# The first weight block of a gated mix of a long convolution and a bilinear unit, brought in as two transfers instead of one

## The chip, the cores and the metric

The kernel runs on one core of a Trainium2 chip. The metric is the device time of one execution in microseconds (us); lower is better. The kernel before was run three times: median 587.12 us, from 586.51 to 587.54.

The core has TensorE (PE, matrix products, with the weight loads shown apart as PEld), VectorE (DVE), ScalarE (ACT), GpSimd (POOL) and SyncE (SP, which mostly issues transfers). Transfers issued by SP, ACT and POOL run on 16 shared DMA engines.

## The reference

For 2048 tokens of 512 channels the reference mixes two branches with a gate per token:

```python
x = A_u
g = _sigmoid((x * gate_w).sum(-1, keepdims=True))
a = _A_ref(x, ...)      # long convolution: y = irfft(rfft(u) * rfft(K)) + u * D_skip
b = _B_ref(x, B_w_gate, B_w_up, B_w_down)
...
g = jnp.einsum("bsd,df->bsf", x, w_gate)
u = jnp.einsum("bsd,df->bsf", x, w_up)
h = g * u
return jnp.einsum("bsf,fd->bsd", h, w_down)
...
return g * a + (1 - g) * b
```

Branch a is a convolution over the whole sequence, with a filter K computed from state-space parameters. Branch b is a bilinear gated unit with 1792 hidden channels. The change concerns the start of branch b.

## The kernel before

**Precision by three products.** TensorE works in a rounded 32-bit format. Each operand is therefore split into a high part (a cast by ACT) and a low part (operand minus high part, by DVE), and each product is three matmuls: high by high, high by low, low by high. `THREE` (line 578) gives their order; for the very first block it is reversed (line 584), so that high by high comes first, then high weights by low tokens (`whi`, `xs`), then low weights by high tokens (`wlo`, `xs`).

**Tiling of branch b.** The 512 channels are four pieces of 128 (`KT` = 4, index `kt`), the 1792 hidden channels are 14 blocks of 128 (index `f`, in four groups), the tokens are four chunks of 512. For a block and a chunk, `hidden` (line 596) forms the gate product in the bank `pg` and the up product in the bank `pu`, each over four values of `kt`. ACT copies `pg` out, DVE multiplies it with `pu` into `h`, ACT and DVE split `h` into `hh` and `hl`, and `down` multiplies these with the down weights into `y`. Transforms for branch a (banks `k`) are fitted between these matmuls, and DVE and ACT compute the tables of the filter meanwhile.

**The start.** `first_loads` (line 492) issues the first transfers. For each `kt` it loads a token tile of 128 channels by 512 tokens (256 KB, into the tile `y`, on SP's queue) and the 128 gate columns and 128 up columns of block 0 that belong to this `kt` (128 KB together, into the tile `ev`, as one transfer). For `kt` = 0 this weight transfer is issued from ACT's queue (line 504), for the others from SP's. Next come the weights of blocks 1 and 2. TensorE meanwhile runs matmuls on zeros (line 514).

`tokens` (line 560) and `first_split` (line 538) turn these into operands. For each `kt`, ACT casts the token tile (512 columns) and then the gate and up weights together (256 columns), and DVE makes the two low parts in the same way. In block 0 the products run by `kt`, gate and up in turn (line 605): `pg` for `kt` = 0 is the first real product of the kernel. `product` (line 580) names the parts of the weight tiles on which it depends, `("k", kt)` for block 0.

**What sets the order.** Nothing is issued as it is written down. Each call of `add` (line 229) makes a task with an engine, an assumed duration in us, the tiles read and written, a rank, an earliest time `after` and, for transfers, a size in KB. `Work.run` (line 301) is a list scheduler: again and again it takes the task that can start first by its own reckoning (ties by rank, then by the order of the calls), and writes the instructions down in that order. Each engine then executes in exactly this order (`InOrder`, line 116) and waits where data are late. For transfers the reckoning uses one shared bus of 0.33 KB per ns, 0.9 us before a transfer begins and 1.0 us until it has landed (lines 214 to 217). A transfer that is issued holds one of a limited number of completion counters; one that finds none free waits on its queue.

Of the kernel before, what the change touches and what calls it, by code (L numbers as in the profile page):

```python
# [10 lines left out]
F32 = mybir.dt.float32  # L11
# [3 lines left out]
ALU = mybir.AluOpType  # L15
# [3 lines left out]
P = 128  # L19
# [150 lines left out]
class Bus:  # L170
# [18 lines left out]
    def add(self, task, at, us):  # L189
        at = max(at, self.now)  # L190
        self.serve(self.queues, self.now, at)
        self.now = at
        self.queues[task.engine == "pool"].append([task, us])
        return self.serve([[[*x] for x in q] for q in self.queues], at, 1e9)
# [170 lines left out]
def gated_mix_kernel(  # L365
# [16 lines left out]
    pe, dve, act, sp, pool_q = (InOrder(tc, e) for e in (nc.tensor, nc.vector, nc.scalar, nc.sync, nc.gpsimd))  # L382
# [3 lines left out]
    add = work.add  # L386
# [18 lines left out]
    def new(pool, tag, shape, dtype=F32, bufs=1, loose=False):  # L405
        return work.tile(pools[pool], tag, shape, dtype, bufs, loose)

    def bank():
        return new("ps_k", "k", [P, D], bufs=4, loose=True)
# [38 lines left out]
    raws = {}  # L448
# [32 lines left out]
    def load_two(key, tile_of, src, one=True):  # L481

        t = tile_of([P, 2, D])
        for k in range(2):
            raws[key(k)] = (t, k)
        if one:
            add("sp", 0.42, lambda: sp.dma_start(t.t, src), w=[t], dma=512, rank=-1)
        return t

    ws, wd, xs = {}, {}, {}  # L490

    def first_loads():
        in_y = lambda shape: new("mid", "y", shape, bufs=2)
        in_ev = lambda shape: new("mid", "ev", shape, bufs=2)
        in_in = lambda shape: new("mid", "in", shape, bufs=2)
        xsrc = lambda kt: xT[P * kt : P * kt + P, :D]
        w0 = raws["w0"] = in_ev([P, 2, D])
        xt = [load_two(lambda k, n=n: ("x", 0, 0, 2 * n + k), in_y, None, False) for n in range(2)]
        wsrc = wts[0][:, : 2 * D].rearrange("p (k d) -> p k d", k=2)
        for kt in range(KT):  # L500

            t, k, ks = xt[kt // 2], kt % 2, slice(P * kt, P * kt + P)
            add("sp", 0.42, lambda t=t, k=k, kt=kt: sp.dma_start(t.t[:, k], xsrc(kt)), w=[(t, k)], dma=256, rank=-1)
            e, q = ("sp", sp) if kt else ("act", act)
            add(e, 0.42, lambda q=q, ks=ks: q.dma_start(w0.t[:, :, ks], wsrc[:, :, ks]), w=[(w0, ("k", kt))], dma=128, rank=-1)
        for f in (1, 2):
            load_two(lambda k, f=f: ("w", f, k), in_ev if f == 1 else in_in, wts[f][:, : 2 * D].rearrange("p (k d) -> p k d", k=2))


        zero = new("glu", "acc", [P, D], bufs=3)  # L510
        scratch = bank()
        add("dve", 0.2, lambda: dve.memset(zero.t, 0.0), w=[zero], rank=-1)

        def warm():
            for _ in range(2):
                pe.matmul(scratch.t, zero.t[:, :P], zero.t, start=True, stop=True)

        add("pe", 3.4, warm, r=[zero], w=[scratch], rank=-1)

    def weights(fs):  # L520
        for f in fs:
            ws[f] = [new("glu", n, [P, 2 * D], F32R, SLOTS) for n in ("whi", "wlo")]
            if f == 0:
                for kt in range(KT):
                    first_split(kt)
                    if kt + 1 < KT:
                        tokens(0, 0, kt + 1)
                continue
            for c in range(2):
                load(("w", f, c), wts[f][:, c * D : (c + 1) * D])  # L530
                if f in GROUPS[0]:
                    split(*ws[f], c, ("w", f, c))
                else:
                    high(ws[f][0], c, ("w", f, c))
            if f not in GROUPS[0]:
                rest(*ws[f], wts[f][:, : 2 * D], 2)

    def first_split(kt):

        hi, lo, t, k = *ws[0], raws["w0"], ("k", kt)  # L540
        cut = lambda x: x.rearrange("p (c d) -> p c d", c=2)[:, :, P * kt : P * kt + P]
        src = lambda: t.t[:, :, P * kt : P * kt + P]
        add("act", 0.38, lambda: act.copy(cut(hi.t), src()), r=[(t, k)], w=[(hi, k)], rank=0)
        add(
            "dve", 0.42,
            lambda: dve.tensor_tensor(out=cut(lo.t), in0=src(), in1=cut(hi.t).bitcast(F32), op=ALU.subtract),
            r=[(t, k), (hi, k)], w=[(lo, k)], rank=0,
        )

    def down_weights(fs):  # L550
        for f in fs:
# [27 lines left out]

    def product(pg, which, w, x, kt, after, first):  # L580
        base = which * D + kt * P
        part = ("k", kt) if first else which

        three = THREE[::-1] if first else THREE

        def fn():
            for n, (a, b) in enumerate(three):
                pe.matmul(
                    pg.t, w[a].t[:, base : base + P], x.t[:, b], start=kt == 0 and n == 0, stop=kt == KT - 1 and n == 2
                )  # L590

        add("pe", 0.681, fn, r=[(w[0], part), (w[1], part), x], w=[pg], rank=2, after=after)
# [3 lines left out]
    def hidden(f):  # L596

        pg = [new("ps_g", n, [P, D]) for n in ("pg", "pu")]
        x = dict(xs)
        after = T_STEP * len(steps) - 5.0  # L600
        steps.append(f)
        pairs = [(which, kt) for which in range(2) for kt in range(KT)]
        if f == 0:

            pairs.sort(key=lambda p: p[1])
        for which, kt in pairs:
            product(pg[which], which, ws[f], x[kt], kt, after, not steps[1:] and f == 0)
        h = new("glu", "h", [P, D])
        hh, hl = (new("glu", n, [P, D], F32R, SLOTS) for n in ("hh", "hl"))
        add("act", 0.59, lambda: act.copy(h.t, pg[0].t), r=[pg[0]], w=[h], rank=0)  # L610
        add(
            "dve", 0.69, lambda: dve.tensor_tensor(out=h.t, in0=pg[1].t, in1=h.t, op=ALU.mult),
            r=[pg[1], h], w=[h], rank=0,
        )
        add("act", 0.62, lambda: act.copy(hh.t, h.t), r=[h], w=[hh], rank=0)
        add(
            "dve", 0.69,
            lambda: dve.tensor_tensor(out=hl.t, in0=h.t, in1=hh.t.bitcast(F32), op=ALU.subtract),
            r=[h, hh], w=[hl], rank=0,
        )  # L620
        return hh, hl
# [391 lines left out]
    def x_table(b):  # L1013

        x, ri, (su, di) = xtab[b], ris[b], sus[b]
        ps = new("tab", "ps", [P, TB, 4])
        lead = [(x, ("l", k)) for k in range(3)]
        tt(0.26, lambda: ps.t, lambda: x.t[:, 0, :, 0:4], lambda: x.t[:, 1, :, 0:4], ALU.add, lead, [ps])
        outer(
            x, lambda: x.t[:, :, :, 0:4], lambda: ps.t, lambda: ri.t[:, :, :, W_M],  # L1020
            lambda: su.t[:, :, W_M], lambda: di.t[:, :, 4:11], [*lead, ps, ri, su, di],
        )
        return x
# [384 lines left out]


    first_loads()  # L1410
    prologue()
    for t in range(NR // 4):
# [7 lines left out]
    x = x_table(0)  # L1420
    for b in range(NB):
# [5 lines left out]
        if b + 1 < NB:  # L1427
            direct_powers(b + 1)
            leads(b + 1)
            x = x_table(b + 1)  # L1430
# [59 lines left out]
```

## Time and profile before

| | |
|---|---|
| median of the runs | 587.12 us |
| lowest, highest of three | 586.51, 587.54 us |
| the profiled execution, its own time | 588.43 us |
| span of the profiled execution | 586.6 us |
| TensorE busy | 576.4 us (98%) |
| VectorE busy | 511.3 us (87%) |
| ScalarE busy | 399.0 us (68%) |
| GpSimd busy | 113.4 us (19%) |
| moved by DMA | 136.28 MB, mean 232 GB/s |

The profile is of one execution. Its span runs from the first to the last instruction that the profiler recorded; the device time is a little longer. The chain of waits is followed back from the last instruction, at each step to what released it. In the timeline, each row gives start, duration, engine, line, operation, output and inputs, and in brackets how long the engine sat idle before and what ended that. Nearly all instructions are recorded at line 124, the helper that issues them, so they are told apart by their tiles: `xs` are token operands (high and low part in one tile), `whi` and `wlo` the high and low weights, `ev` the raw weights of the first blocks, `y` at the start the raw token tiles (later it is also the name of other buffers, among them the results of `down`).

### The profile page before, as it was taken

What the parts mean: (1) busy time and instruction counts of PE and PEld (TensorE: products, weight loads), DVE (VectorE), ACT (ScalarE), POOL (GpSimd) and SP (SyncE); (2) the same over time, 40 slices, a digit from 0 to 9 for tenths busy, and PEclk for the clock granted to TensorE, in tenths of its full rate; (3) what the DMA queues carried; (4) which work ended last, traced back from release to release, by engine and by line L of the source; (5) the groups of instructions that cost most, each with busy time, mean ns of one, the idle gap of its engine ahead of it and who ended that gap; (6) DMA issues with size and microseconds to landing.
All of it is one profiled execution on the core that took longest, in us unless ns stands there. A gap on an engine that the chain in (4) does not pass through costs nothing.

```text
span 586.6 us, 14827 instructions
## 1 busy us (share of the span) xinstructions
PE 576.4 (98%) x5996; PEld 433.9 (74%) x5996; DVE 511.3 (87%) x812; ACT 399.0 (68%) x891; POOL 113.4 (19%) x159
## 2 busy tenths in 40 slices
PE   8999999999989999999999999999999999999997
PEld 5777777877876777887777778777878787677775
DVE  6998999999999999999799999995999982367664
ACT  5468888898578589876968764899696523443351
POOL 0002222311102231310412200421321104011011
PEclk9999999999999999999999999999999999999999
DMA  8999969997647698998697859899958349899976
GB/s 276 383 369 357 374 241 319 289 257 212 125 154 181 194 272 205 228 245 297 135 257 249 183 180 304 158 187 276 221 136 212 65 143 230 290 270 253 283 159 125
DMA packets 71687, 136.28 MB, mean 232 GB/s; under 512 B 6852, under 2 KB 35780, under 8 KB 69188
## 3 DMA queue, kind: packets, MB, share of 16 engines
q1 hardware_dynamic: 47668, 87.10, 43.0%
q0 software_dynamic: 23392, 47.98, 39.5%
q8 instruction: 47, 0.77, 0.6%
q10 hardware_dynamic: 560, 0.26, 0.2%
q14 instruction: 20, 0.16, 0.1%
HBM read 80.27 MB, written 55.05 MB: 231 GB/s over the span
## 4 chain that ended last, share of the span: by engine, by line
PE 83%; DVE 6%; ACT 4%; DMA 4%; issue 1%; SPq 0%; DVEq 0%; ACTq 0%
PE pg L124 23%; PE pu L124 23%; PE y L124 22%; PE k L124 16%; DVE v L124 1%; DMA pb<-par_d 1%; DMA xs_d<-xs 1%; DVE x L124 1%; DMA y<-in_xT 1%; DMA xs<-xs_d 1%; ACT acc L124 1%; DVE t L124 1%; ACT ev L124 1%; ACT xs L124 1%; ACT e L124 1%
## 5 line engine op out<-in xcount | busy, mean ns | idle before, releaser
L124 PE MATMUL pg<-xs,whi 128*128 128x512 f32 x448 | 138.9, 391 | 1.0 <-DVE xs L124 0.6
L124 PE MATMUL pu<-xs,whi 128*128 128x512 f32 x448 | 138.3, 390 | 0.0
L124 PEld LDWEIGHTS pg<-xs,whi 128*128 128x128 f32 x448 | 84.2, 188 | 20.2 <-ACT whi L124 2.0
L124 PEld LDWEIGHTS pu<-xs,whi 128*128 128x128 f32 x448 | 84.2, 188 | 16.9
L124 PE MATMUL y<-dhi,hl 128*128 128x512 f32 x224 | 90.3, 403 | 2.9 <-DVE hl L124 2.4
L124 PE MATMUL pu<-xs,wlo 128*128 128x512 f32 x224 | 90.1, 402 | 0.0
L124 PE MATMUL pg<-xs,wlo 128*128 128x512 f32 x224 | 89.4, 399 | 0.4 <-ACT h L124 0.4
L124 PE MATMUL y<-dlo,hh 128*128 128x512 f32 x224 | 87.5, 391 | 0.0
L124 PE MATMUL y<-dhi,hh 128*128 128x512 f32 x224 | 87.3, 390 | 0.0
L124 POOL DMA_DIRECT2D out<-acc x44 | 40.2, 968 | 180.4 <-ACT acc L124 173.0
L124 ACT COPY ev<-k 128x512 f32<-128x512 f32 x112 | 58.8, 596 | 14.5 <-PE k L124 14.4
L124 ACT CAST hh<-h 128x512 fp32r<-128x512 f32 x56 | 34.6, 618 | 45.7 <-DVE h L124 45.5
L124 PEld LDWEIGHTS y<-dhi,hl 128*128 128x128 f32 x224 | 42.0, 187 | 24.4 <-issue 8.1
L124 DVE TENSOR_TENSOR h<-pu,h 128x512 f32<-128x512 f32 x56 | 38.5, 688 | 23.6 <-PE pu L124 23.0
L124 PEld LDWEIGHTS pu<-xs,wlo 128*128 128x128 f32 x224 | 42.0, 187 | 20.0 <-issue 10.7
L124 ACT ACTIVATE acc<-y,ngate 128x512 f32<-128x512 f32 x62 | 41.7, 685 | 21.9 <-PE y L124 18.9
L124 PEld LDWEIGHTS pg<-xs,wlo 128*128 128x128 f32 x224 | 42.1, 188 | 18.4 <-issue 6.9
L124 ACT COPY h<-pg 128x512 f32<-128x512 f32 x56 | 32.9, 587 | 28.3 <-PE pg L124 22.0
L124 PEld LDWEIGHTS y<-dhi,hh 128*128 128x128 f32 x224 | 42.1, 188 | 9.1
L124 PEld LDWEIGHTS y<-dlo,hh 128*128 128x128 f32 x224 | 42.1, 188 | 8.2 <-DVE dlo L124 0.3
L124 DVE TENSOR_TENSOR hl<-h,hh 128x512 fp32r<-128x512 f32 x56 | 38.4, 686 | 3.0 <-ACT hh L124 2.7
L124 PEld LDWEIGHTS k<-v,x 128*32 128x32 f32 x2048 | 30.6, 109 | 6.4 <-issue 4.7
(130 smaller groups left out, 965.4 us busy)
## 6 DMA issues: line engine op xcount, KB each, us to landing
xs<-xs_d SPq DMA_DIRECT2D x36, 512.0 KB, 5.8
out<-acc POOLq DMA_DIRECT2D x44, 256.0 KB, 5.9
raw<-in_wts SPq DMA_DIRECT2D x33, 256.0 KB, 5.6
xs_d<-xs SPq DMA_DIRECT2D x16, 512.0 KB, 6.6
su_d<-ev POOLq DMA_DIRECT2D x32, 256.0 KB, 6.3
y_d<-ts SPq DMA_DIRECT2D x28, 256.0 KB, 4.9
in<-su_d POOLq DMA_DIRECT2D x12, 512.0 KB, 5.9
sk_d<-ev SPq DMA_DIRECT2D x6, 1024.0 KB, 5.4
```

Of the source, the lines that this page charges most:

```text
L124: got = getattr(self.engine, name)(*args, **kw)
```

## The change

For `kt` = 0 the transfer of 128 KB from ACT's queue is replaced by two of 64 KB. The gate columns are issued first, from ACT's queue; the token tile follows from SP's queue; the up columns come behind it, from SP's queue too. The values of `after` (0.0, 0.1, 0.2) fix this order for the planner. Each of the two halves has its own cast on ACT (128 columns, assumed 0.27 us) and its own low part on DVE (128 columns, assumed 0.29 us), and the products of `kt` = 0 depend on their own half only. For `kt` = 1 to 3 everything is as before.

```diff
         for kt in range(KT):
...
-            add("sp", 0.42, lambda t=t, k=k, kt=kt: sp.dma_start(t.t[:, k], xsrc(kt)), w=[(t, k)], dma=256, rank=-1)
-            e, q = ("sp", sp) if kt else ("act", act)
-            add(e, 0.42, lambda q=q, ks=ks: q.dma_start(w0.t[:, :, ks], wsrc[:, :, ks]), w=[(w0, ("k", kt))], dma=128, rank=-1)
+            x_in = lambda t=t, k=k, kt=kt: sp.dma_start(t.t[:, k], xsrc(kt))
+            if kt == 0:
+                for c in range(2):
+                    e, q = ("sp", sp) if c else ("act", act)
+                    add(
+                        e, 0.42, lambda q=q, c=c, ks=ks: q.dma_start(w0.t[:, c, ks], wsrc[:, c, ks]),
+                        w=[(w0, ("k", kt, c))], dma=64, rank=-1, after=0.2 * c,
+                    )
+                    if c == 0:
+                        add("sp", 0.42, x_in, w=[(t, k)], dma=256, rank=-1, after=0.1)
+                continue
+            add("sp", 0.42, x_in, w=[(t, k)], dma=256, rank=-1)
+            add("sp", 0.42, lambda ks=ks: sp.dma_start(w0.t[:, :, ks], wsrc[:, :, ks]), w=[(w0, ("k", kt))], dma=128, rank=-1)
...
-        hi, lo, t, k = *ws[0], raws["w0"], ("k", kt)
-        cut = lambda x: x.rearrange("p (c d) -> p c d", c=2)[:, :, P * kt : P * kt + P]
-        src = lambda: t.t[:, :, P * kt : P * kt + P]
-        add("act", 0.38, lambda: act.copy(cut(hi.t), src()), r=[(t, k)], w=[(hi, k)], rank=0)
...
+        hi, lo, t = *ws[0], raws["w0"]
+        for c in [slice(0, 2)] if kt else [slice(0, 1), slice(1, 2)]:
+            k = ("k", kt) if kt else ("k", kt, c.start)
+            cut = lambda x, c=c: x.rearrange("p (c d) -> p c d", c=2)[:, c, P * kt : P * kt + P]
+            src = lambda c=c: t.t[:, c, P * kt : P * kt + P]
+            add("act", 0.38 if kt else 0.27, lambda cut=cut, src=src: act.copy(cut(hi.t), src()), r=[(t, k)], w=[(hi, k)], rank=0)
+            add(
+                "dve", 0.42 if kt else 0.29,
+                lambda cut=cut, src=src: dve.tensor_tensor(
+                    out=cut(lo.t), in0=src(), in1=cut(hi.t).bitcast(F32), op=ALU.subtract
+                ),
+                r=[(t, k), (hi, k)], w=[(lo, k)], rank=0,
+            )
...
-        part = ("k", kt) if first else which
+        part = which if not first else ("k", kt) if kt else ("k", kt, which)
```

More of the change, by code (lines that the diff above doesn't have):

```diff
@@ L538, in first_split @@
     def first_split(kt):
-        hi, lo, t, k = *ws[0], raws["w0"], ("k", kt)
-        cut = lambda x: x.rearrange("p (c d) -> p c d", c=2)[:, :, P * kt : P * kt + P]
-        src = lambda: t.t[:, :, P * kt : P * kt + P]
-        add("act", 0.38, lambda: act.copy(cut(hi.t), src()), r=[(t, k)], w=[(hi, k)], rank=0)
[L544 to L548, printed above, removed]
+        hi, lo, t = *ws[0], raws["w0"]
[11 more added lines that the diff above has]
+            )
     def down_weights(fs):
```

## The prediction

> **What bounds the kernel now.** I read the page first, for the engine that fills the span and for the share of the chain that ended last.
>
> ```profile
> span 586.6 us, 14827 instructions
> ...
> PE 576.4 (98%) x5996; PEld 433.9 (74%) x5996; DVE 511.3 (87%) x812; ACT 399.0 (68%) x891; POOL 113.4 (19%) x159
> ...
> PE 83%; DVE 6%; ACT 4%; DMA 4%; issue 1%; SPq 0%; DVEq 0%; ACTq 0%
> ```
>
> TensorE is busy for 98% of the span and carries 83% of the chain. A change at the very start can therefore pay only by letting the dense part of TensorE's work begin earlier, and only if no later wait eats the lead. So I went to the chain in order of time, over the first 70 us, to see what the dense part hangs on.
>
> ```profile
> 0.74 3.95 DMA y<-in_xT
> ...
> 5.69 1.45 PE pg L124 x3
> 7.14 0.69 PE pu L124 x3
> ```
>
> The chain begins with the first token tile (`y<-in_xT`), which lands 3.95 us after its issue, and reaches the first three matmuls at 5.69. These take 1.45 us, the next three 0.69: there are 0.76 us of slack in the first triple, and the first block's gate and up weights are what the change touches. The timeline of the first microseconds shows the instructions (start, duration, engine, operation, and in brackets the idle time before).
>
> ```profile
> 0.74 0.47 ACTq L124 DMA_DIRECT2D ev<-in_wts  x1
> ...
> 0.74 0.86 SPq L124 DMA_DIRECT2D y<-in_xT  x2
> ...
> 1.66 0.43 SPq L124 DMA_DIRECT2D ev<-in_wts  x1
> ...
> 2.12 0.47 SPq L124 DMA_DIRECT2D y<-in_xT  x1
> ...
> 2.63 0.43 SPq L124 DMA_DIRECT2D ev<-in_wts  x1
> ...
> 3.11 0.47 SPq L124 DMA_DIRECT2D y<-in_xT  x1
> ...
> 4.71 0.62 ACT L124 CAST xs<-y 128x512 fp32r<-128x512 f32 x1 [1.68 <-DMA y<-in_xT]
> 5.08 0.89 SPq L124 DMA_DIRECT2D ev<-in_wts  x2
> 5.24 0.40 ACT L124 CAST whi<-ev 128x256 fp32r<-128x256 f32 x1
> 5.36 0.69 DVE L124 TENSOR_TENSOR xs<-y,xs 128x512 fp32r<-128x512 f32 x1 [3.80 <-ACT xs L124]
> ...
> 5.81 0.62 ACT L124 CAST xs<-y 128x512 fp32r<-128x512 f32 x1 [0.17 <-DMA y<-in_xT]
> 5.97 0.42 DVE L124 TENSOR_TENSOR wlo<-ev,whi 128x256 fp32r<-128x256 f32 x1
> ...
> 6.46 0.69 DVE L124 TENSOR_TENSOR xs<-y,xs 128x512 fp32r<-128x512 f32 x1
> ```
>
> ACT casts the token tile (4.71 to 5.33), then gate and up weights together (5.24 to 5.64), and TensorE starts at 5.69. DVE makes the tokens' low part (5.36 to 6.05) and then the weights' low part (5.97 to 6.39). Because each product runs high by high, high weights by low tokens, low weights by high tokens, the second matmul needs the tokens' low part. The timeline of TensorE in narrow windows gives the single instructions.
>
> ```profile
> 5.69 0.80 PE L124 MATMUL pg<-xs,whi 128*128 128x512 f32 x1 [0.45 <-ACT whi L124]
> 6.11 0.29 PEld L124 LDWEIGHTS pg<-xs,whi 128*128 128x128 f32 x1
> 6.28 0.62 PE L124 MATMUL pg<-xs,whi 128*128 128x512 f32 x1
> 6.44 0.28 PEld L124 LDWEIGHTS pg<-xs,wlo 128*128 128x128 f32 x1
> 6.71 0.43 PE L124 MATMUL pg<-xs,wlo 128*128 128x512 f32 x1
> 6.98 0.40 PE L124 MATMUL pu<-xs,whi 128*128 128x512 f32 x1
> ```
>
> The second weight load starts at 6.11, 0.06 after the tokens' low part is finished (6.05); the third at 6.44, 0.05 after the weights' low part (6.39). The matmuls start at 6.28, 6.71 and 6.98: spaced 0.43, then 0.27 us.
>
> **The change, part by part.** *First matmul.* It needs the gate's high part and the tokens' high part, and no longer the up half. The sizes of one cast on ACT are 0.62 for 512 columns and 0.40 for 256, so an estimate for 128 is 0.40 - 0.11 = 0.29; on DVE, 0.69 and 0.42 give 0.42 - 0.135, again 0.29. If the gate's cast is out of the way when the token tile lands, TensorE starts 0.04 after 5.33, at 5.37: 0.32 earlier.
>
> *Second matmul.* Its weight load still waits for 6.05, hence 6.11, and the start is still 6.28. The 0.32 us are thus gained in front of a wait that the change does not touch: worth 0. *Third matmul.* Its low part is now ready early, but the matmul follows the second by 0.43, and its weight load at 6.44 lay before 6.71 already: worth 0, unless the array takes its faster pace sooner. If the spacings 0.43 and 0.27 both became the 0.23 of the three-matmul step (0.69 / 3), that would be 0.20 + 0.04 = 0.24 us. Bounds 0 to -0.24; I take 0, since the row at 6.11 does not move.
>
> [...]
>
> *ACT's order.* The order is fixed by the planner. By its constants (0.33 KB per ns, 0.9 to start, 1.0 to land) the gate half is planned to land ahead of the token tile, so its cast is put in front of the token cast. Whether that is free depends on when the gate half really lands. The transfers of the two queues in the first 3.5 and the first 4.25 us, and landing times counted from the issue:
>
> ```profile
> q1 hardware_dynamic: 134, 0.26, 38.1%
> q10 hardware_dynamic: 117, 0.06, 6.6%
> ...
> q1 hardware_dynamic: 210, 0.39, 41.3%
> q10 hardware_dynamic: 265, 0.12, 10.7%
> ...
> ev<-in_wts ACTq DMA_DIRECT2D x1, 128.0 KB, 4.3
> ```
>
> q10 is ACT's queue, q1 SP's. By 3.5 us SP's queue had moved about the first token tile (0.26 MB) and ACT's 117 packets, 0.06 MB: the size of the new gate half. So the gate half would finish with the token tile, not well ahead of it. If it lands 0.29 before 4.69 its cast is free; if together, it puts off the token cast by 0.29 less the 0.09 by which ACT's instructions overlap (4.71 + 0.62 against 5.24), 0.20; at the latest it lands where the whole 128 KB did, 0.74 + 4.3 = 5.04, and the delay is 0.35 + 0.20 = 0.55. All of this passes through the tokens' low part to the second matmul. I take +0.1, between "just ahead" and "together".
>
> *The up half, and the second cast and low part.* The extra cast costs 2 x 0.29 - 0.40 = 0.18 on ACT, and 0.16 on DVE. ACT's part falls before 4.71 (idle 1.68) and between 5.24 and 5.81 (idle 0.17); DVE's first part in its 3.80 of idle time, its second ends 0.13 earlier than the present 6.39, before 6.46. Nothing waits longer: 0. If the cover were gone, it would be 0.18.
>
> *The issue moved onto SP.* One more issue of 0.43 goes between the first token tile and the second, so that every later transfer on SP is issued later. Byte for byte the queues carry the same, and the second token tile still follows the same 384 KB. There is one hard wait, though: after the issue at 3.11 SP pauses until 5.08.
>
> ```profile
> SPq L124 <- DMA ev<-in_wts: 1.9, 2, 1.5
> ...
> DMA to landing us min/median/max: 3.4/4.5/4.8
> ```
>
> The longest of these waits, 1.5, is this pause, and it ends 0.04 after the first weights land (5.04). Six transfers on SP and two on ACT had been issued: the ninth waits for the first. With the extra transfer the ninth is no longer the fourth weights but the fourth token tile. Its issue moves from 3.11 to about 4.7 (the first landing). What that costs is not in the trace; the weights' landing times bound it: 4.7 + 3.4 = 8.1, or 4.7 + 4.8 = 9.5.
>
> ```profile
> 8.14 0.62 ACT L124 CAST xs<-y 128x512 fp32r<-128x512 f32 x1 [0.17 <-DMA y<-in_xT]
> ...
> 9.53 0.42 DVE L124 TENSOR_TENSOR wlo<-ev,whi 128x256 fp32r<-128x256 f32 x1
> ...
> 10.62 0.19 PEld L124 LDWEIGHTS pg<-xs,wlo 128*128 128x128 f32 x1
> ```
>
> Today that tile's cast starts at 8.14; the last product that hangs on it is ready at 9.95 and needed at 10.62. So 0.67 us of lateness is covered; 1.4 late would cost 0.7. Bounds 0 to +0.7. The fourth weights were issued at 5.08, with the same queue ahead, and met the shortest landing at the earliest; I take 0.
>
> [...]
>
> *The order behind it.* The planner decides every later step by comparing start times; some change by a few hundredths to 0.4 us, so neighbours can change places far behind the start. The places where TensorE stood idle show what that can be worth.
>
> ```profile
> 26.86 0.73 PE L124 MATMUL pg<-xs,whi 128*128 128x512 f32 x2 [0.57 <-DVE xs L124]
> ...
> 142.35 0.50 PE L124 MATMUL y<-dhi,hl 128*128 128x512 f32 x1 [0.74 <-DVE hl L124]
> ...
> 173.91 0.50 PE L124 MATMUL y<-dhi,hl 128*128 128x512 f32 x1 [1.63 <-DVE hl L124]
> ...
> 20.00:142.00 122.00, 120.21 (x842) 89.94 (x840) 118.45 (x201) 101.09 (x228) 25.31 (x41) 1.00 0.92 305
> ```
>
> From 20 to 142 us TensorE is busy for 120.21 of 122 and DVE (third figure) for 118.45. A lead of tenths can vanish in any of these three waits, and the largest, 1.63, is the size of what one changed place can open or close. Bounds -1.63 to +1.63; I take 0, having no row for either sign.
>
> *Sum:* 0 + 0 + 0.1 + 0 + 0 + 0 = +0.1 us. The profiled execution took 588.43 (span 586.6 and 1.83 around it), 1.31 above the median of the runs, 587.12. So 588.5 profiled, and a median of 587.2.
>
> **The rivals.** *A, the early start is kept:* the gate half lands early, and the whole 0.32 stays, because the second matmul is not held by the tokens' low part. For it: the second matmul also comes one 0.43 step after the first's streaming began. Against it: the row at 6.11. Time 587.12 - 0.32 = 586.8. *B, the start gets worse:* the gate half lands last (+0.55), or the fourth token tile comes late (+0.7); one of the two, 587.7 to 587.8. For it: the packet counts, and the pause on SP. Against it: the 0.67 of cover. *C, faster:* the new order closes the wait at 173.91. For it: it is a wait for one DVE step, which the order places. Time 587.2 - 1.63 = 585.6. *D, slower:* the new order opens another such wait. The place is a low part of the hidden values (`hl`) behind another DVE step, while DVE is full and TensorE has nothing else in its fixed order; it decides as soon as that step is later than the last matmul ahead of it, as at 142.35 and 173.91. Price up to 1.63: 588.8. Against C and D: a change of a few tenths may leave the order nearly as it was.
>
> **How the numbers follow.** The forecast gets 0.43, A 0.12, B 0.12, C 0.15, D 0.18; D gets a little more than C since two such waits have arisen where DVE is full. About 0.2%, 1.17 us, is what a measurement of this kernel can tell from no change. The forecast, A and B lie within it: same 0.67, faster 0.15, slower 0.18. The range goes from C's 585.6 to D's 588.8, which takes in the bounds of the start; of C and D the outer part, some 0.2, lies outside.
>
> **What would show it right or wrong.** Right: the first matmul near 5.4 to 5.6 while the second stays at 6.2 to 6.5; two casts and two low parts of 0.29 for the first weights; SP's pause in front of the fourth token tile instead of the fourth weights; the first block's last matmul within 0.3 of where it was. Wrong: a second matmul before 6.1 (A); a weight load at 10.6 or later that waits (B); a TensorE wait for `hl` that is gone (C) or new (D) by over 1 us.

## The result, and the profile after

The changed kernel took 591.07 us (median of 7 runs, 589.85 to 595.52) against 587.54 us for the kernel before in the same comparison (7 runs, 586.51 to 590.66): ratio 1.0056, 95% interval 1.003 to 1.0083. By the ratio it is slower by about 3.3 us, by the medians by 3.5: outside the range on record, and well beyond 0.2%.

The page of the changed kernel, in the lines that answer to those of before:

```profile
span 590.7 us, 14832 instructions
...
PE 576.9 (98%) x5996; PEld 435.1 (74%) x5996; DVE 512.1 (87%) x813; ACT 400.1 (68%) x892; POOL 113.6 (19%) x159
...
PE 80%; DVE 9%; ACT 5%; DMA 3%; issue 1%; SPq 0%; DVEq 0%; ACTq 0%
...
L124 PE MATMUL pg<-xs,wlo 128*128 128x512 f32 x224 | 90.5, 404 | 4.5 <-ACT h L124 4.5
```

TensorE is busy for 576.9 us, 0.5 more than before; the span is 4.1 longer. So TensorE mostly waits longer, and the last row says for what: 4.5 us in front of `pg` products, for `h`, ACT's copy that empties the bank `pg`. In the page of before the same row was:

```profile
L124 PE MATMUL pg<-xs,wlo 128*128 128x512 f32 x224 | 89.4, 399 | 0.4 <-ACT h L124 0.4
```

The timeline of the first microseconds shows the first of these waits grow:

```profile
0.74 0.86 SPq L124 DMA_DIRECT2D y<-in_xT  x2
...
1.66 0.90 SPq L124 DMA_DIRECT2D ev<-in_wts  x2
...
4.51 0.33 SPq L124 DMA_DIRECT2D y<-in_xT  x1
4.52 0.30 ACT L124 CAST whi<-ev 128x128 fp32r<-128x128 f32 x1 [1.56 <-DMA ev<-in_wts]
...
5.16 0.62 ACT L124 CAST xs<-y 128x512 fp32r<-128x512 f32 x1 [0.34 <-DMA y<-in_xT]
...
5.83 0.50 PE L124 MATMUL pg<-xs,whi 128*128 128x512 f32 x1 [0.62 <-ACT xs L124]
5.88 0.61 ACT L124 CAST xs<-y 128x512 fp32r<-128x512 f32 x1
...
6.55 0.50 PE L124 MATMUL pg<-xs,whi 128*128 128x512 f32 x1 [0.23 <-DVE xs L124]
...
9.22 0.62 ACT L124 CAST xs<-y 128x512 fp32r<-128x512 f32 x1 [1.59 <-DMA y<-in_xT]
...
12.03 1.14 ACT L124 CAST whi<-ev 128x512 fp32r<-128x512 f32 x2 [1.78 <-DMA ev<-in_wts]
...
13.30 1.14 ACT L124 CAST whi<-in 128x512 fp32r<-128x512 f32 x2
14.35 0.58 ACT L124 COPY h<-pg 128x512 f32<-128x512 f32 x1
...
14.97 0.54 PE L124 MATMUL pg<-xs,wlo 128*128 128x512 f32 x1 [2.83 <-ACT h L124]
```

Four things are to be seen. First, SP issues **two token tiles** before the up part. The first cast of tokens starts at 5.16 instead of 4.71, the second at 5.88 without any wait: the second tile was there already. The description of the change ahead of the prediction says that `after` fixes the order gate, token tile, up part. That is wrong. The second token tile has no earliest time, so the scheduler takes it at 0.0, ahead of the first with its 0.1. Second, the fourth token tile is the ninth transfer, issued at 4.51, and its cast starts at 9.22 (8.14 before). Third, block 1's weights (`ev`, 512 columns) are cast from 12.03 and block 2's (`in`) from 13.30. Fourth, ACT copies `pg` only behind block 2's casts, at 14.35, and TensorE stands for 2.83 us. Before, the same three steps were:

```profile
9.80 1.14 ACT L124 CAST whi<-ev 128x512 fp32r<-128x512 f32 x2 [0.74 <-DMA ev<-in_wts]
11.27 0.59 ACT L124 COPY h<-pg 128x512 f32<-128x512 f32 x1 [0.33 <-PE pg L124]
11.75 1.14 ACT L124 CAST whi<-in 128x512 fp32r<-128x512 f32 x2
```

The copy stood ahead of block 2's casts. In the scheduler's own reckoning the two plans end at the same time, so it foresaw no loss. It reckoned the first token tile, and with it the first products and the copy, later than before; block 2's weights it reckoned as early as before, so their casts could start first. In the stretches behind the wait TensorE is also slower; the third figure from the right is the granted clock.

```profile
12.00:14.00 2.00, 0.15 (x1) 0.00 (x0) 1.32 (x3) 1.84 (x4) 0.00 (x0) 1.00 1.02 400
14.00:16.00 2.00, 1.03 (x3) 0.88 (x4) 1.93 (x6) 0.92 (x2) 0.00 (x0) 0.82 1.06 387
16.00:18.00 2.00, 2.00 (x6) 1.51 (x6) 2.00 (x8) 0.62 (x1) 0.00 (x0) 0.50 1.02 407
18.00:20.00 2.00, 2.00 (x9) 1.60 (x8) 2.00 (x7) 0.38 (x1) 0.00 (x0) 0.82 0.99 388
```

It is 0.50 from 16 to 18 us and, in stretches of half a microsecond, from 15.5 to 18.5. Three matmuls take 1.28 us there (16.17 to 17.45), and 0.68 after it (19.42 to 20.10). TensorE's lag (how much later the same product starts than in the kernel before) grows over this stretch, from 3.06 us at the mark at 14.97 (11.91 before) to 4.62 at the product at 24.86 (20.24 before). Three of the seven executions, this one among them, had a mean granted clock of 0.997 and took 592.51 to 595.52; the other four, at 0.999 and 1.0, took 589.85 to 591.07. These four are still slower than before, so the drop of the clock is not the whole loss.

Further on, TensorE's waits of over half a microsecond are these:

```profile
58.31 0.50 PE L124 MATMUL y<-dhi,hl 128*128 128x512 f32 x1 [0.70 <-DVE hl L124]
72.81 0.50 PE L124 MATMUL pg<-xs,wlo 128*128 128x512 f32 x1 [0.76 <-ACT h L124]
...
177.64 0.50 PE L124 MATMUL y<-dhi,hl 128*128 128x512 f32 x1 [0.62 <-DVE hl L124]
333.98 0.39 PE L124 MATMUL y<-dhi,hl 128*128 128x512 f32 x1 [0.72 <-issue]
340.12 0.48 PE L124 MATMUL k<-y,w3s 32*64 32x128 f32 x16 [0.75 <-issue]
431.77 0.50 PE L124 MATMUL pg<-xs,wlo 128*128 128x512 f32 x1 [0.87 <-ACT h L124]
```

At 177.64 (the same product stands at 173.91 before) the lag is 3.73. The wait of that product was 1.63 before and is 0.62 now: the gain that rival C of the prediction hoped for is there, and the end comes no earlier. Behind that, before had one wait of 0.63, at 493.00; now there are three of 0.72 to 0.87. At the last of them, 431.77, the product that stands at 426.68 before, the lag is 5.09; a few products earlier, at 422.44 (418.38 before), it was 4.06.

### The profile page after: what moved, and what is told of

It is laid out like the page before. It is cut to its first block, busy times and chain, and to the rows that moved or that the text cites. A ratio compares the mean times of both kernels' runs of the same rounds, so it can differ in the third digit from the quotient of the medians.

```text
span 590.7 us, 14832 instructions
## 1 busy us (share of the span) xinstructions
PE 576.9 (98%) x5996; PEld 435.1 (74%) x5996; DVE 512.1 (87%) x813; ACT 400.1 (68%) x892; POOL 113.6 (19%) x159
## 4 chain that ended last, share of the span: by engine, by line
PE 80%; DVE 9%; ACT 5%; DMA 3%; issue 1%; SPq 0%; DVEq 0%; ACTq 0%
PE pg L124 23%; PE y L124 22%; PE pu L124 21%; PE k L124 15%; DVE v L124 2%; DMA raw<-in_wts 1%; DMA in<-in_wts 1%; DVE x L124 1%; DVE t L124 1%; DVE hl L124 1%; DVE ri L124 1%; ACT L124 1%; DVE y L124 1%; DVE h L124 1%; ACT ev L124 1%
```

## The experiments

**Theory A**: the loss comes from the written order. The second token tile goes first, which delays the start and makes the scheduler write another order for everything behind. **Rival B**: it comes from the one transfer more, which makes the ninth wait for the first and delays all weights behind it. A second rival is that the late first tile itself costs, not the order written for it. (The letters A and B in the expectations mean these two, not the rivals of the prediction.) Ratios are against runs of the kernel before on the same chip, with 95% intervals.

**The token tile first.** The description's order, with one edit:

```diff
-                        add("sp", 0.42, x_in, w=[(t, k)], dma=256, rank=-1, after=0.1)
+                        add("sp", 0.42, x_in, w=[(t, k)], dma=256, rank=-1)
```

> The change with the first token tile at the earliest time 0.0 instead of 0.1, so that the list scheduler issues it ahead of the second token tile, as the description has it (in the changed kernel the second tile went first, because it has no earliest time). Theory A (the loss comes from the scheduler's order: second token tile first, and with it the copy of pg behind the casts of block 2's weights on ACT): the copy stands ahead of these casts again, TensorE's wait at about 15 us (2.83) shrinks to under 1, and the time is within 1 us of before. Rival B (the loss comes from the one transfer more: the ninth has to wait for the first to land, so the fourth token tile and all behind it are late): block 1's weights still land near 12 instead of 9.8, TensorE still loses 1.5 us or more there, and the time stays 2 us or more above before.

Measured: 588.52 us against 588.91, ratio 1.0000 (0.9985 to 1.0016). The timeline:

```profile
0.74 0.39 SPq L124 DMA_DIRECT2D y<-in_xT  x1
...
1.19 0.42 SPq L124 DMA_DIRECT2D ev<-in_wts  x1
...
1.65 0.42 SPq L124 DMA_DIRECT2D y<-in_xT  x1
...
4.04 0.30 ACT L124 CAST whi<-ev 128x128 fp32r<-128x128 f32 x1 [1.10 <-DMA ev<-in_wts]
4.24 0.61 ACT L124 CAST xs<-y 128x512 fp32r<-128x512 f32 x1
...
5.64 0.50 PE L124 MATMUL pg<-xs,whi 128*128 128x512 f32 x1 [0.22 <-DVE xs L124]
...
11.04 1.14 ACT L124 CAST whi<-ev 128x512 fp32r<-128x512 f32 x2 [0.91 <-DMA ev<-in_wts]
12.08 0.57 ACT L124 COPY h<-pg 128x512 f32<-128x512 f32 x1
...
12.56 1.14 ACT L124 CAST whi<-in 128x512 fp32r<-128x512 f32 x2
12.71 0.50 PE L124 MATMUL pg<-xs,wlo 128*128 128x512 f32 x1 [0.87 <-ACT h L124]
```

The up part is behind the first tile, the copy is ahead of block 2's casts, and the whole loss is gone. The second matmul waits for the tokens' low part (the row at 5.64), as the prediction had it. Here block 1's weights are late too (11.04), so B's delay is real, but it costs 0.87 us at 12.71 and nothing at the end. In the two timelines TensorE's products stand in the order of before, one by one; in the changed kernel they do not.

**The exchange alone**, in the kernel before: an earliest time for the first token tile, nothing else.

```diff
-            add("sp", 0.42, lambda t=t, k=k, kt=kt: sp.dma_start(t.t[:, k], xsrc(kt)), w=[(t, k)], dma=256, rank=-1)
+            add("sp", 0.42, lambda t=t, k=k, kt=kt: sp.dma_start(t.t[:, k], xsrc(kt)), w=[(t, k)], dma=256, rank=-1, after=0.0 if kt else 0.1)
```

> The kernel before with one edit: the first token tile gets an earliest time of 0.1, so that the second goes ahead of it. As many transfers as before, no split. Theory A: the same order on ACT as in the changed kernel (the copy of pg behind block 2's casts); TensorE starts some 0.5 to 0.9 later and waits 1 to 3 us for that copy; 589 to 591 us. Rival B: block 1's weights land near 9.8 as before, and the time is within 1 us of before.

Measured: 590.23 us, ratio 1.0026 (1.0011 to 1.0041). No split, no ninth transfer, and still about half of the loss (the ratios are 1.0026 and 1.0056, with intervals that overlap). Block 1's weights were cast from 9.66, so the weights were not late, and the copy of `pg` stood behind block 2's casts again. A's prediction of 1 to 3 us lost at that copy was a miss: ACT had finished the casts before the bank was full, and the copy waited for TensorE. But in this profiled execution TensorE ran at half its pace until about 9.8 us (more on this at the hidden split), so the bank filled late; what the copy's place costs at full pace does not show here. (In the profile of the order alone, below, at full pace, TensorE waited 0.47 us for this copy at 12.73.) The longest wait of this profile is a later one for a copy of `pg`, 1.87 us at 429.81.

**The ninth transfer alone**, in the kernel before: 2 KB more on ACT's queue, unknown to the scheduler.

```diff
+        def two_small():
+            act.dma_start(small[:, 0], rows[1].rearrange("(p c) -> p c", c=KT))
+            act.dma_start(extra, rows[1].rearrange("(p c) -> p c", c=KT))
```

> The kernel before with one more transfer of 2 KB on ACT's queue, issued inside the task that loads the small table, so that the scheduler's order is unchanged. Its data are not used. Theory A: within 1 us of before, since the order is that of before. Rival B: the fourth token tile is the ninth transfer and is issued near 4.7 instead of 3.11, DMA moves under 150 GB/s for a microsecond near 7, block 1's weights land near 12, TensorE waits 1.3 to 2 us for their low part, and the time is 588.5 to 589.5.

Measured: 588.03 us, ratio 0.9985 (0.997 to 1.0001). The fourth token tile waits, as B says, and it cost nothing. SP's queue in the timeline:

```profile
2.63 0.43 SPq L124 DMA_DIRECT2D ev<-in_wts  x1
5.03 0.33 SPq L124 DMA_DIRECT2D y<-in_xT  x1
```

And TensorE's wait for block 1's low part, with a later mark:

```profile
12.28 0.47 PE L124 MATMUL pg<-xs,wlo 128*128 128x512 f32 x1 [0.56 <-DVE wlo L124]
...
142.23 0.50 PE L124 MATMUL y<-dhi,hl 128*128 128x512 f32 x1 [0.73 <-DVE hl L124]
```

The fourth token tile goes out at 5.03 instead of 3.11, TensorE loses 0.56 at 12.28, and at 142.23 it is level with before (142.35). The weights were less late than B had it, though: block 1's were cast from 10.50, not near 12 (9.80 before, 12.03 in the changed kernel). What refutes B alone is this run together with the token tile first (11.04, ratio 1.0000) and with the last experiment (11.87, ratio 1.001): later weights, and no clear loss.

**The copy of `pg` ahead again**, in the changed kernel: block 2's casts may not start before 10.4 by the scheduler's reckoning (`split` passes an `after` on to its cast).

```diff
-                    split(*ws[f], c, ("w", f, c))
+                    split(*ws[f], c, ("w", f, c), 10.4 if f == 2 else 0.0)
```

> The changed kernel with one edit: the casts of block 2's weights get an earliest time of 10.4, so that the copy of pg stands ahead of them on ACT again. The second token tile still goes first, and the ninth transfer still waits. If the wait at 14.97 is the queue on ACT (block 2's weights land at 13.3 and the copy stands behind their casts until 14.35), TensorE can go on when block 1's low part is made, near 13.4, and about 1.5 us of the wait of 2.83 go: 1 to 2 us below the changed kernel. If it is only the late weights, nothing is gained. Both together (late weights and order) leave it at 588.5 to 589.5.

Measured: 590.93 us, ratio 1.0028 (1.0014 to 1.0042), against 1.0056 and, in another comparison (below), 1.0046 for the changed kernel. The wait near 15 was gone from the profile. The ratio fits the forecast of 1 to 2 us, but its interval overlaps with those of the changed kernel, and the order behind was rewritten once more (the wait near 430 is gone too). In this profile TensorE also ran at half its pace until about 11 us, and there the copy waited 0.79 us for the bank. So the run does not show what the copy's place costs, and where its own loss arises stays open.

**The changed kernel once more**, unedited.

> The changed kernel once more, beside the others of this call. Expected 1.004 to 1.008 of before; its first product waits for the first token tile, which goes second on SP's queue, and TensorE waits 2 to 3 us near 15 for the copy of pg behind block 2's casts.

Measured: 591.43 us against 588.54, ratio 1.0046 (1.0026 to 1.0066). The wait for the copy was 1.69 us here, without a drop of the granted clock behind it. Eight of the 12 executions had a mean granted clock of 0.999 or 1.0 and took 590.70 to 591.84: the loss is there without the drop.

**The exchange hidden from the scheduler**: the tasks keep their places, but the first issues the second tile and the second the first.

```diff
-            add("sp", 0.42, lambda t=t, k=k, kt=kt: sp.dma_start(t.t[:, k], xsrc(kt)), w=[(t, k)], dma=256, rank=-1)
+            j = 1 - kt if kt < 2 else k
+            add("sp", 0.42, lambda t=t, j=j, kt=kt: sp.dma_start(t.t[:, j], xsrc(kt - kt % 2 + j)), w=[(t, k)], dma=256, rank=-1)
```

> The kernel before, with the first two token tiles exchanged inside their tasks: SP issues the second tile, then the first, but the list scheduler does not know and writes the order of before for everything else. Theory A (the written order costs, not the late tile): TensorE starts 0.4 to 0.8 late, the copy of pg stays ahead of block 2's casts, and the time is within 1 us of before. Rival (the late tile itself costs): 589 us or more, as with the exchange that the scheduler sees, whose ratio was 1.0026.

Measured: 589.63 us, ratio 1.0018 (0.9997 to 1.0039): unclear. **The split hidden from the scheduler**, both halves, casts and low parts inside the old tasks (the casts, for one):

```diff
-        add("act", 0.38, lambda: act.copy(cut(hi.t), src()), r=[(t, k)], w=[(hi, k)], rank=0)
+        cs = [slice(0, 2)] if kt else [slice(0, 1), slice(1, 2)]
+        def high_parts():
+            for c in cs:
+                act.copy(cut(hi.t, c), src(c))
+        add("act", 0.38, high_parts, r=[(t, k)], w=[(hi, k)], rank=0)
```

> The kernel before, with the first weights split into two transfers (both from ACT's queue), two casts and two low parts inside the same tasks: the written order of everything else is that of before, token tile first. Theory A: within 1 us of before; one transfer more makes the fourth token tile the ninth, so block 1's weights land 0.5 to 1.5 late, and that lag is gone by 142 us. Rival B (the split itself costs): 1 us or more above before.

Measured: 589.10 us, ratio 1.0016 (0.9994 to 1.0039): unclear as well. Its profile shows one thing in which executions differ. TensorE in the first block:

```profile
7.18 1.05 PE L124 MATMUL pu<-xs,whi 128*128 128x512 f32 x2
8.04 0.63 PE L124 MATMUL pu<-xs,wlo 128*128 128x512 f32 x1
8.46 1.05 PE L124 MATMUL pg<-xs,whi 128*128 128x512 f32 x2
9.32 0.63 PE L124 MATMUL pg<-xs,wlo 128*128 128x512 f32 x1
9.74 0.84 PE L124 MATMUL pu<-xs,whi 128*128 128x512 f32 x2
```

Three matmuls take 1.28 us (8.04 to 9.32), and not 0.69: the array keeps half its pace until about 10, where in the profile of before it gained its full pace before 7. The lag that arises, about 1.5 us, is still there at 175.42 (173.91 before). It does not show in the span, 586.5 us against 586.6; part of the reason is that the profile of before stands idle for 0.63 us at 493.00, as no other profile does, and lags read against it shrink by about 1 us there. Four profiles stayed at half pace beyond 9 us: these two, the exchange alone and the copy ahead. Whether these kernels do so more often than before was not tried; so the two do not decide between theory and rival.

**Three matmuls on zeros instead of two**, in the kernel before:

```diff
-            for _ in range(2):
+            for _ in range(3):
                 pe.matmul(scratch.t, zero.t[:, :P], zero.t, start=True, stop=True)
```

> The kernel before with three matmuls on zeros ahead of the first product instead of two, unknown to the scheduler: TensorE's first real product starts about 1.2 us later (one such matmul took 1.7 us, and 0.45 us were idle), and the order is unchanged. If the start carries through the dense part, the end is 1 to 1.3 later. If a lead or lag at the start is taken up by the waits for VectorE up to 174 us (as the 0.45 us of lag at 69 us were gone at 142 with the ninth transfer alone), the lag is under 0.3 at 174 us and the time within 0.5 us of before.

Measured: 587.78 us, ratio 0.9981 (0.9963 to 0.9999). The first product came at 5.93, only 0.24 later, not 1.2; part of the added matmul filled the 0.45 us of idle time. So the run says little on a late start. What it shows is the scatter: 586.62 to 588.68 over 12 runs, against 586.33 to 592.2 over 35 of the kernel before. (More runs make a range wider; the standard deviations, 0.61 and 1.44 us, differ too.) A repetition:

> The kernel before with three matmuls on zeros instead of two, once more: its first product had come only 0.24 us later, not 1.2, and without a gap. Expected 0.997 to 1.000 of before; if the three matmuls keep TensorE at its full pace in the first block in every execution, the times scatter less than those of before.

Measured: 588.28 us, ratio 0.9992 (0.9976 to 1.0007), 587.7 to 589.69. The narrower scatter came again; a gain in the median is not settled, and that the half pace at the start is the cause of the scatter is not shown.

**The order alone.** The counterpart of the hidden exchange: the scheduler plans the second tile first and writes the order for it, but the tasks exchange the two tiles back.

```diff
-            add("sp", 0.42, lambda t=t, k=k, kt=kt: sp.dma_start(t.t[:, k], xsrc(kt)), w=[(t, k)], dma=256, rank=-1)
+            j = 1 - kt if kt < 2 else k
+            add("sp", 0.42, lambda t=t, j=j, kt=kt: sp.dma_start(t.t[:, j], xsrc(kt - kt % 2 + j)), w=[(t, k)], dma=256, rank=-1, after=0.0 if kt else 0.1)
```

> The kernel before, with the first token tile planned at 0.1, so that the list scheduler writes the order that it wrote with the exchange alone; but inside the tasks the two tiles are exchanged back, so that the first token tile really is issued first. Written order new, landings as before. Theory (about half of the loss is the written order behind the start, with the wait for the copy of pg near 430 us): 1.001 to 1.004 of before, lag at 175 us under 0.5, the wait near 430 of 1.5 to 2 us there. Rival (all of the loss arises in the first 15 us): within 0.1% of before.

Measured: 590.18 us against 588.45, ratio 1.0024 (1.0003 to 1.0044), as much as the visible exchange cost, though the interval reaches down into the rival's 0.1%. Its profile decides more sharply, though it is of one execution (589.09 us): the lag is 0.21 at 174.12 (173.91 before), both kernels start the same product at 418.38, and then comes a wait near 430, of 1.35 where the theory had 1.5 to 2. The timeline there:

```profile
424.51 0.62 ACT L124 CAST dhi<-raw 128x512 fp32r<-128x512 f32 x1 [3.17 <-DMA raw<-in_wts]
425.04 0.61 ACT L124 CAST hh<-h 128x512 fp32r<-128x512 f32 x1
...
427.55 0.59 ACT L124 COPY h<-pg 128x512 f32<-128x512 f32 x1 [1.89 <-DVE hl L124]
428.19 0.50 PE L124 MATMUL pg<-xs,wlo 128*128 128x512 f32 x1 [1.35 <-ACT h L124]
```

The same place in the kernel before:

```profile
424.65 0.59 ACT L124 COPY h<-pg 128x512 f32<-128x512 f32 x1 [1.03 <-DVE hl L124]
425.80 0.62 ACT L124 CAST dhi<-raw 128x512 fp32r<-128x512 f32 x1 [0.55 <-DMA raw<-in_wts]
...
426.68 0.39 PE L124 MATMUL pg<-xs,wlo 128*128 128x512 f32 x1
```

In the new order a cast of raw down weights stands ahead of `hh` on ACT and waits 3.17 us for their transfer; `hh`, the low part and the copy of `pg` queue behind it, and TensorE waits 1.35. Before, the copy came first, and the same product started at 426.68: 1.51 us are lost here, in one step, with the first tile issued first and no transfer more.

**The changed kernel with the tiles exchanged back** in the same way: its order, one transfer more, but the first tile lands first.

```diff
-            x_in = lambda t=t, k=k, kt=kt: sp.dma_start(t.t[:, k], xsrc(kt))
+            j = 1 - kt if kt < 2 else k
+            x_in = lambda t=t, j=j, kt=kt: sp.dma_start(t.t[:, j], xsrc(kt - kt % 2 + j))
```

> The changed kernel with its written order, but with the first two token tiles exchanged back inside their tasks, so that the first lands first. The copy of pg still stands behind block 2's casts and one transfer more is in flight. Theory (the copy's place and the order behind it cost, the late first tile hardly): 1.003 to 1.006 of before, a wait of 1.5 us or more for the copy of pg near 14. Rival (the late first tile is the cause): within 0.2% of before.

Measured: 590.64 us, ratio 1.0037 (1.0015 to 1.0059), with a wait of 1.00 us for the copy near 13.4, where the theory had 1.5 or more. The ratio speaks against the late first tile as the main cause; the interval reaches down into the rival's 0.2%, so this run alone does not exclude it.

**The token tile first, with three matmuls on zeros** (both edits shown above):

> The split with the first token tile first (measured 1.000 of before), and three matmuls on zeros ahead of the first product instead of two, so that TensorE has no gap before its first product. If the start of TensorE counts, 0.997 to 0.999 of before; if waits behind it take up the lead, 1.000.

Measured: 589.1 us, ratio 1.001 (0.9995 to 1.0025). No version was found that beats the kernel before beyond doubt.

## Why the prediction was wrong

**The step that failed** is "One more issue of 0.43 goes between the first token tile and the second". I read the order from the description and the values of `after`, and did not run the list scheduler's rule by hand for the one task without such a value. The rule is that the earliest start wins, and rank and place count only in a tie: 0.0 for the second tile beats 0.1 for the first. With it failed the term "The order behind it", taken at 0: the order that the scheduler wrote for this start costs about 1.7 us by itself (590.18 against 588.45, with a wide interval). With the token tile first the forecast holds: ratio 1.0000, where it said +0.1 us; an interval of 0.15% either way says nothing of tenths, so the single small terms are not confirmed by it.

**The first and second matmul.** Right in mechanism: with the tile first, the second waits for the tokens' low part. It came at 5.64 and not at 6.28, since the tile's cast started at 4.24, 0.47 earlier than before; by the prediction's own sign (before 6.1) that spoke for rival A, but the lead was gone at 12.71 and worth nothing. The +0.1 for ACT's order can't be told from nothing in the times. The gate's cast did stand ahead of the tile's by 0.20 (4.04 and 4.24, and 4.75 and 4.95 with three matmuls on zeros), and the tile's followed without a wait for its transfer: this is the price of "together", 0.20, at most. The latest landing that I allowed, 5.04, was no bound: in the changed kernel with the tiles exchanged back the gate's cast started only at 5.29.

**The transfer that became the ninth.** Right that it is held: issue at 4.51, tile cast at 9.22, 1.08 later than before, where I had 0 to 1.4 and counted 0.67 as covered; no wait of TensorE for this tile of half a microsecond or more appears. The step stopped one link short. Behind the tile lie block 1's and block 2's weights (cast from 12.03 instead of 9.80, from 13.30 instead of 11.75), and I gave no price for what hangs on them.

**The order behind it.** Here I took 0 with bounds of 1.63 either way. Two waits of this kind arose, and both for ACT's copy of `pg` and not, as rival D of the prediction said, for `hl`: 2.83 and 1.69 us near 14 in two profiles of the changed kernel, and 0.58 to 1.87 near 430 in the kernels with its order. The largest wait in the trace was no bound for a new one. C and D were also not alternatives: the same order shortened the wait at 173.91 from 1.63 to 0.61 or 0.62 and opened these.

**What the runs share out.** The order alone gives 1.0024, the exchange 1.0026, the full change 1.0046 and 1.0056. All comparisons of kernels with a new order of TensorE's products (these, the tiles exchanged back and the copy ahead) have intervals above 1; of those that keep the order of before, with a split, a late tile or a ninth transfer, none has. So the loss hangs on the written order above all; that the late tile or the split costs a little besides (1.0018 and 1.0016, both unclear) is not excluded. The part above the 1.0024 came with the copy's wait near 14, late weights and order together; the intervals overlap too much to put a figure on each. The drop of the granted clock is not the main part, since executions without it are as slow (590.70 to 591.84); what it adds to the others stays open.

## What to carry to other kernels

Where a scheduler writes the order, a new earliest time on one task moves every task that has none; list the planned starts of all rivals for the queue before pricing anything. A step of hundredths at the start can be worth nothing on the critical path and still cost microseconds, since the order of all that follows is drawn anew: look for in-order queues in which a step that waits for a transfer stands ahead of the copy that frees a bank. To tell the written order from the data, exchange the data inside the tasks, once with and once without the plan.

## What the runs showed of the hardware

A TensorE wait of 2.83 us was followed by a granted clock of 0.82, 0.50 and 0.82 in three stretches of 2 us; the waits of 1.87, 1.69 and 1.63 in other profiles were not followed by such a drop.

At the start, behind two matmuls on zeros (3.78 us), the first block gained its full pace before 7 us in the profile of before, but only near 10 us in the profile of the hidden split, which has the same two matmuls. The granted clock of these stretches reads 1.00 in both, so at the start this figure does not show the pace; the spacing of the matmuls does (0.43 and 0.23 us). What sets the moment at which the pace rises was not shown.

DMA moved little behind SP's pause. In the changed kernel, in the stretches of the windows view, the last figures are busy share and GB/s:

```profile
7.00:8.00 1.00, 1.00 (x6) 0.83 (x5) 1.00 (x3) 0.63 (x2) 0.00 (x0) 1.00 0.65 114
```

The same stretch of the kernel before, in which the fourth token tile had been issued 1.4 us earlier:

```profile
7.00:8.00 1.00, 1.00 (x6) 0.83 (x5) 0.87 (x4) 0.93 (x2) 0.00 (x0) 1.00 1.07 362
```

The pause on SP, 1.0 us from 3.5 to 4.5, was shorter than the slow stretch that followed: in the three stretches from 6 to 9 us the engines moved 235, 114 and 230 GB/s, where before they moved 356, 362 and 410. In the stretch shown, 122 of 144 packets were under 2 KB, against 140 of 221 before. Whether that is the reason was not tried.
